# Scoring the third layer's sliding window in 64-row blocks, and unread matmuls in the last layer

## The chip, the cores and the metric

The kernel runs on one core of a Trainium2 chip. The metric is the device time of one launch in microseconds. A core has engines with queues of their own that run side by side: TensorE (PE) multiplies matrices and writes PSUM, ScalarE (ACT) evaluates the exponential here and reads PSUM, VectorE (DVE) does the elementwise work, GpSimd (POOL) and SyncE (SP) mostly issue transfers. An engine takes its instructions in program order; semaphores make one wait for another. [...]

## The reference

Four attention layers on one sequence of 2048 tokens of width 640, 32 heads of 20 elements. Layers 0 and 2 (the first and third) see a window of 256 keys, layers 1 and 3 (the second and last) see all keys:

```python
def attend(x, wqkv, wo, mask):            # mask is None in layers 1 and 3
    q, k, v = split_heads(x @ wqkv)       # 32 heads, Dh = 20
    s = einsum("bhqd,bhkd->bhqk", q, k) * Dh ** -0.5
    if mask is not None: s = where(mask, s, -1e9)
    return join_heads(softmax(s) @ v) @ wo
idx = arange(2048)
window = (idx[:, None] - idx[None, :] >= 0) & (idx[:, None] - idx[None, :] < 256)
x = x + attend(layernorm(x), A_wqkv, A_wo, window)    # layer 0
x = x + attend(layernorm(x), B_wqkv, B_wo, None)      # layer 1
x = x + attend(layernorm(x), A_wqkv, A_wo, window)    # layer 2
x = x + attend(layernorm(x), B_wqkv, B_wo, None)      # layer 3
```

## The kernel before

The queries are cut into four chunks `c` of 512, the heads into eight groups `g` of four. A `Unit(l, c, g)` is the attention of one layer, chunk and head group; the head `j` of a group lies on partitions 32j to 32j+19. A unit is a list of banks. A bank is one PSUM bank of scores, 128 keys by up to 512 queries of one head: keys are on the partitions, queries on the columns. `window_banks(c)` lists the banks of a windowed unit: three for each head, each filled by two score matmuls, of which one takes an early key block and the other a late one. For c > 0 all three are 512 columns wide (1536 columns a head); for c = 0 they have 512, 384 and 256 (1152).

Units of different layers follow each other in a fixed interleaved list. The eight units of layer 2 for a chunk stand, two at a time, between units of layer 1 of the next chunk; those of layer 2's last chunk stand between units of layer 3. The first part of layer 3, chunk 0, begins there; chunks 1 to 3 of layer 3 stand alone at the end, 24 units.

The main loop makes a "tile" of three banks (at times two or four) in each turn. For tile t it emits, in this order:

1. the score matmuls (line 1308) into one of two sets of PSUM banks, 0 to 2 for even tiles and 3 to 5 (with 6 for a tile of four banks) for odd ones;
2. the exponentials (line 1339), one ACTIVATE for each run of banks that begin at the same column, from PSUM to a bf16 tile `pt`;
3. other work by credit: `pump` advances generators for layer norm, projections (lines 364 and 465), output projection (line 552) and softmax normalisation, at a pace that `rate(t)` takes from due times counted in tiles; the pace is a number of TensorE microseconds a tile;
4. `keep_clock`: as long as the "heat" of the turn (matmuls of such other work) is under `state["least"]`, it emits an unread matmul, `unread` (line 634) into bank 6, or, when that bank is taken, "owes" one that goes ahead of the next tile's scores into its bank (line 1302). It multiplies the identity with a mask and nobody reads what it writes. `least` is 1.76 for a tile of three banks from layer 1 on, and zero from unit (3, 1, 0) on;
5. the products with the values (line 1373) for four banks of an earlier tile, accumulated in bank 7;
6. a step of the "side": some banks of layers 1 and 3 have their exponential evaluated by VectorE from polynomials (lines 910 to 941), at a pace of `SIDE_RATE` or 0.4 VectorE microseconds a tile;
7. the multiplication by 0/1 masks of the previous tile's windowed banks (line 1410, VectorE).

Tile t+1's scores go into the set that tile t-1's exponential has to release, while ACT works on tile t. `fill` in `t_tail` (line 1030) emits unread matmuls at the very end.

## Time and profile before

| what | value |
|---|---|
| time, median of 3 runs | 2285.77 us (2281.72 to 2287.35) |
| profiled span | 2282.3 us |
| ACT busy | 2169.6 us, 95% |
| PE busy | 1978.4 us, 87% |
| DVE busy | 1272.2 us, 56% |
| exponentials, line 1339 | 2096.5 us, 1638 recorded |
| unread matmuls, line 634 | 243.5 us, 708 recorded, none after 1653 us |
| window masks on DVE, line 1410 | 209.5 us, 403 recorded |

Busy time of an engine is the time in which at least one of its instructions was running; PE overlaps matmuls, so a busy PE isn't one at its peak. A few per cent of the matmuls can be missing from the records. PEclk is the share of TensorE's full clock that was granted.

### The profile page before, as it was taken

To read this page: it belongs to the slowest core of one execution; us is meant where nothing else is said; L and a number is where in the kernel's file an instruction comes from. 1 tells how busy PE (TensorE), PEld (TensorE's weight loads), DVE (VectorE), ACT (ScalarE), POOL (GpSimd) and SP (SyncE) were. 2 spreads that over 40 slices of the span, in tenths; PEclk is the share of its full clock that TensorE was granted. 3 is DMA by queue.
4 is the path that set the end of the run, shared out by engine and by line. 5 is a ranking of instruction groups with operands and counts; after the bars stand their busy time and mean duration, and the time that the engine had idled before them with its cause. 6 is when DMAs were issued, how large, how long until landed. Compare 5 with 4: busy or idle time off the path is not lost.

```text
span 2282.3 us, 40030 instructions
## 1 busy us (share of the span) xinstructions
PE 1978.4 (87%) x15586; PEld 704.1 (31%) x15746; DVE 1272.2 (56%) x2214; ACT 2169.6 (95%) x1741; POOL 271.0 (12%) x445
## 2 busy tenths in 40 slices
PE   8899999989898998888888998898878888888887
PEld 3343343333233333233332333232221122122222
DVE  6667675435454566455564643432555565666662
ACT  7789899999999999999899999999999999999997
POOL 4323223201100122001210022011000000000000
PEclk9899999999999999999999999999755565556556
DMA  6223223322210233002320043012111111111100
GB/s 193 78 69 101 81 83 90 97 75 56 70 33 14 61 96 93 15 27 64 101 71 14 16 116 95 28 44 74 54 47 30 30 42 30 30 39 41 35 17 15
DMA packets 88284, 135.16 MB, mean 59 GB/s; under 512 B 20766, under 2 KB 63486, under 8 KB 88094
## 3 DMA queue, kind: packets, MB, share of 16 engines
q1 hardware_dynamic: 68878, 79.43, 12.6%
q0 software_dynamic: 19216, 53.17, 7.8%
q8 instruction: 123, 2.02, 0.4%
q14 instruction: 67, 0.55, 0.1%
HBM read 99.52 MB, written 27.79 MB: 56 GB/s over the span
## 4 chain that ended last, share of the span: by engine, by line
ACT 45%; PE 30%; issue 16%; DVE 9%; DMA 0%; ACTq 0%; POOL 0%; SPq 0%; DVEq 0%; POOLq 0%
ACT pt L1339 44%; PE ps L1308 7%; PE ps L364 6%; PE ps L552 5%; PE ps L1373 4%; PE ps L465 3%; DVE pt L1410 2%; PE ps L634 1%; DVE st L314 1%; DVE on L1085 1%; ACT ka L1339 1%; PE ps L1081 1%; DVE x_sb L561 1%; PE ps L429 0%; DVE raw_o L910 0%
## 5 line engine op out<-in xcount | busy, mean ns | idle before, releaser
L1339 ACT ACTIVATE pt<-ps 128x1536 bf16<-128x1536 f32 (+2 forms) x1638 | 2096.5, 1478 | 74.2 <-PE ps L1308 64.9
L1308 PE MATMUL ps<-qt,kt 32*128 32x512 bf16 x4008 | 635.9, 451 | 176.7 <-ACT pt L1339 144.6
L1373 PE MATMUL ps<-pt,vt 128*21 128x512 bf16 x3852 | 462.5, 452 | 7.1 <-issue 4.5
L1308 PEld LDWEIGHTS <-kt 32*128 32x128 bf16 x4008 | 186.0, 93 | 594.1 <-issue 575.7
L1410 DVE TENSOR_TENSOR pt<-pt,masks 128x1024 bf16<-128x1024 bf16 (+6 forms) x403 | 209.5, 554 | 151.0 <-ACT pt L1339 150.5
L634 PE MATMUL ps<-masks,ident 128*128 128x512 bf16 x708 | 243.5, 387 | 27.7 <-DVE on L1085 7.1
L364 PE MATMUL ps<-xnT,wqk 128*128 128x512 bf16 x761 | 206.3, 382 | 19.2 <-DVE on L1085 3.9
L1373 PEld LDWEIGHTS <-vt 128*21 128x21 bf16 x3960 | 99.5, 90 | 337.4 <-issue 325.1
L314 DVE CAST st<-ps 128x512 bf16<-128x512 f32 x134 | 92.7, 692 | 183.8 <-PE ps L364 169.9
L552 PE MATMUL ps<-wop,on 128*128 128x320 bf16 x928 | 165.0, 317 | 8.3 <-DVE x_sb L561 5.2
L910 DVE TENSOR_SCALAR xnT<-ps 128x512 int32<-128x512 f32 x88 | 60.9, 692 | 185.8 <-PE ps L903 185.8
L1308 PE MATMUL ps<-qa,ka 32*128 32x384 bf16 (+2 forms) x1408 | 118.2, 278 | 27.7 <-ACT pt L1339 22.0
L1085 DVE TENSOR_TENSOR on<-on,ps 128x512 bf16<-128x512 bf16 x128 | 86.4, 685 | 65.8 <-PE ps L1081 64.7
L561 DVE TENSOR_TENSOR x_sb<-x_sb,ps 128x320 bf16<-128x320 bf16 x120 | 58.1, 484 | 115.1 <-PE ps L552 114.9
L857 DVE CAST on<-ps 128x512 bf16<-128x512 f32 x112 | 77.1, 688 | 75.1 <-PE ps L1373 48.3
L465 PE MATMUL ps<-wv,xnT 128*128 128x320 bf16 x640 | 110.6, 301 | 7.9 <-DVE on L1085 3.1
L552 PEld LDWEIGHTS <-on 128*128 128x128 bf16 x928 | 84.0, 101 | 77.0 <-issue 47.8
L364 PEld LDWEIGHTS <-wqk 128*128 128x128 bf16 x830 | 69.9, 97 | 111.3 <-issue 53.9
L634 PEld LDWEIGHTS <-ident 128*128 128x128 bf16 x798 | 59.7, 96 | 132.6 <-issue 131.2
L398 POOL TENSOR_SCALAR rstd<-mv 128x4 f32<-128x4 f32 x15 | 4.1, 277 | 776.6 <-DVE mv L385 755.9
L1373 PE MATMUL ps<-pt,va 128*21 128x384 bf16 (+2 forms) x1408 | 75.6, 282 | 3.9 <-DVE pt L1410 1.6
L1308 PEld LDWEIGHTS <-ka 32*128 32x128 bf16 x1408 | 43.0, 92 | 95.9 <-issue 85.9
(101 smaller groups left out, 1585.1 us busy)
## 6 DMA issues: line engine op xcount, KB each, us to landing
vt<-v_d SPq DMA_DIRECT2D x48, 336.0 KB
kt<-k_d SPq DMA_DIRECT2D x192, 80.0 KB
wqk<-in_B_wqkv_dram POOLq DMA_DIRECT2D x80, 160.0 KB, 3.5
wqk<-in_A_wqkv_dram POOLq DMA_DIRECT2D x70, 160.0 KB, 3.4
k_d<-st POOLq DMA_DIRECT2D x75, 128.0 KB, 2.1
q_d<-st POOLq DMA_DIRECT2D x75, 128.0 KB, 2.1
qt<-q_d SPq DMA_DIRECT2D x384, 20.0 KB
v_d<-vs POOLq DMA_DIRECT2D x16, 336.0 KB, 3.0
```

The source lines that it names most:

```text
L314: nc.vector.tensor_copy(out=out_, in_=in_)
L364: nc.tensor.matmul(pq, lhsT=wt[:, dc, :], rhs=xt[:, dc, :], start=(dc == 0), stop=(dc == KD - 1),)
L465: nc.tensor.matmul(pv, lhsT=xt[:, dc, i * P : (i + 1) * P], rhs=wv_sb[l % 2][:, dc, h * HD : (h + 1) * HD], start=(dc == 0), stop=(dc == K ...
L552: nc.tensor.matmul(yp, lhsT=on[:, g, qb * P : (qb + 1) * P], rhs=wop[:, g, i * HD : (i + 1) * HD], start=(g == a), stop=(g == b - 1),)
L561: nc.vector.tensor_tensor(out=xv, in0=had, in1=yp, op=ALU.add)
L634: nc.tensor.matmul(ps[:, b, :], lhsT=ident[:], rhs=masks[:, 0, :], start=True, stop=True)
L857: nc.vector.tensor_copy(out=oT, in_=op)
L1085: nc.vector.tensor_tensor(out=oT, in0=oT, in1=zb, op=ALU.mult)
L1308: nc.tensor.matmul(sp[:, i, col * P : (col + qn) * P], lhsT=u.k(kc, j), rhs=u.q(j, q0, qn), start=True, stop=True,)
L1339: nc.scalar.activation(out=pt[:, i:k, b0 * P :], in_=sp[:, i:k, b0 * P :], func=ACT.Exp, scale=SCALE,)
L1373: nc.tensor.matmul(op[32 * j : 32 * j + VW, q0 * P : (q0 + qn) * P], lhsT=u.v(kc, j), rhs=pg[:, i, col * P : (col + qn) * P], start=(first ...
L1410: nc.vector.tensor_tensor(out=pt_[:, i:k, cols], in0=pt_[:, i:k, cols], in1=mv_, op=ALU.mult)
```

## The change

Layer 2 alone gets a new list of banks, `windows(c)`. Keys are taken in blocks of 64 instead of 128: in a bank the lower 64 partitions hold one key block and the upper 64 the next one, each with the query columns that it needs, so less of the bank is outside the window. For c > 0 a head has two "fine" banks of 512 columns and one unmasked of 256 (1280 columns); for c = 0 two of 448 and one of 128 (1024). Each score matmul now has 64 key columns as weights and writes 64 partitions, and a lower and an upper one alternate. In a few columns the upper half belongs to other queries than the lower one; `mask` copies those columns, multiplied by a triangle, into a small tile `phi`, and they get value products of their own.

Layer 0 keeps the old banks (`wide_windows`). The heat that a tile must have follows its width in columns and not its number of banks, and no longer ends at the last layer, so unread matmuls go on to the end. They read the identity, repeated four times, instead of a mask. The side's pace goes from 0.85 to 1.05 and from 0.4 to 0.65 a tile. The core of the diff:

```diff
-SIDE_RATE = 0.85
+SIDE_RATE = 1.05
...
+    for n, ge, base in ((0, False, 0), (1, True, 0), (2, True, B), (3, False, -B)):
+        v = tri[:, n, :]
+        nc.gpsimd.affine_select(
...
-            ps[:, b, :], lhsT=ident[:], rhs=masks[:, 0, :], start=True, stop=True
+            ps[:, b, :].rearrange("p (a b) -> p a b", a=4), lhsT=ident[:], rhs=idents,
+            start=True, stop=True,
...
+    def windows(c):
+        found = []
+        for o in range(2):
+            k, q = 4 * c + o, 2 * o
+            low = [(k, q, 5, 1), (k + 2, q + 4, 2, 6)]
+            high = [(k, q + 1, 5, 2), (k + 2, q + 5, 1, 7)]
+            values = [
+                (k, q, 5, 1, False), (k + 2, q + 4, 2, 6, False), (k, q + 5, 1, 6, True),
+            ]
+            if c > 0:
+                low.append((k - 2, q, 1, 0))
+                high.insert(1, (k - 2, q, 2, 0))
+                values = [(k - 2, q, 1, 0, False), *values, (k - 2, q + 1, 1, 1, True)]
+            else:
+                high[0] = (k, q, 6, 1)
+            found.append(((0 if c > 0 else B, C), "fine", low, high, values))
+        pairs = [(4 * c + 2, 6, 2, 0)] + [(4 * c - 1, 0, 2, 2)] * (c > 0)
+        found.append(((0, 2 * B * len(pairs)), None, pairs, pairs, [(*p, False) for p in pairs]))
...
-                for n in range(2):
-                    for i, (u, j, m, b0, subs, first, last, end) in enumerate(cur):
-                        for kc, q0, qn, col in subs[n : n + 1]:
+                for n in range(0, max(len(x) for x in jobs), 2):
+                    for i, x in enumerate(jobs):
+                        for half, lhsT, rhs, col in (job for job in x[n : n + 2] if job):
+                            rows = slice(0, P) if half is None else slice(B * half, B * half + B)
                             nc.tensor.matmul(
-                                sp[:, i, col * P : (col + qn) * P],
-                                lhsT=u.k(kc, j), rhs=u.q(j, q0, qn), start=True, stop=True,
+                                sp[rows, i, col : col + rhs.shape[1]],
+                                lhsT=lhsT, rhs=rhs, start=True, stop=True,
...
-                state["least"] = warmth * n_b / 3 if state["unit"] < index[3, 1, 0, None] else 0.0
+                state["least"] = warmth * width / 3
...
+                if all(b[2] is not None and b[2] != "side" and b[2].masked in ("fine", None) for b in cur):
+                    r *= width / 2.5
...
-                side["credit"] = min(side["credit"] + (SIDE_RATE if side["late"] else 0.4), 1.2)
+                side["credit"] = min(side["credit"] + (SIDE_RATE if side["late"] else 0.65), 1.2)
```

In a tile that mixes banks of layer 2 with banks of layer 1 or 3, the latter are also scored in two halves of 64 keys.

More of the change, by code (lines that the diff above doesn't have):

```diff
@@ L28 @@
 HD = D // 2
+B = 64
 VW = DH + 1
@@ L72 @@
     ptp = pool("ptp", 6)
+    phip = pool("phip", 3)
     stp = pool("stp", 4)
@@ L95 @@
     spread4 = big.tile([64, 4, P], BF16, name="spread4", tag="spread4")
+    tri = big.tile([P, 4, B], BF16, name="tri", tag="tri")
     masks = big.tile([P, 3, C], BF16, name="masks", tag="masks")
@@ L155 @@
         )
+    nc.gpsimd.memset(tri[:], 1.0)
+    for n, ge, base in ((0, False, 0), (1, True, 0), (2, True, B), (3, False, -B)):
+        v = tri[:, n, :]
+        nc.gpsimd.affine_select(
+            out=v, in_=v, compare_op=ALU.is_ge if ge else ALU.is_gt, fill=0.0,
+            base=base, pattern=[[1 if ge else -1, B]], channel_multiplier=-1 if ge else 1,
+        )
+    idents = ident[:].unsqueeze(1).to_broadcast((P, 4, P))
     nc.vector.memset(ka_all[:, G:KA, :], 0.0)
@@ L674, in __init__ @@
             if self.windowed:
-                sets = [(m, b0, subs, j) for m, b0, subs in window_banks(c) for j in range(4)]
+                sets = [(w, w.cols, w.values, j) for w in (windows if l == 2 else wide_windows)(c) for j in range(4)]
             else:
@@ L681, in __init__ @@
                 sets = [
-                    (None, 0, [(kc, 0, 4, 0)], j) for kc in range(k0, k1) for j in range(4)
+                    (None, (0, C), [(kc, 0, C, 0, False)], j)
+                    for kc in range(k0, k1) for j in range(4)
                     if kc < NT - 1 or j not in self.aside
@@ L686, in __init__, with k, scores @@
             self.banks = [
-                (self, j, m, b0, subs, i < 4, i >= n - 4 + len(self.aside), i == n - 1)
-                for i, (m, b0, subs, j) in enumerate(sets)
-            ]
-        def k(self, kc, j):
+                (self, j, w, cols, subs, i < 4, i >= n - 4 + len(self.aside), i == n - 1)
+                for i, (w, cols, subs, j) in enumerate(sets)
+            ]
+        def k(self, kc, j, half=None):
+            o = kc * P
             if self.windowed:
-                t, o = ka[kc // 4, self.g], kc % 4
+                t, o = ka[kc // 4, self.g], o % C
             else:
-                t, o = kt[self.l, self.c, self.g], kc
-            return t[32 * j : 32 * j + 32, o * P : (o + 1) * P]
+                t = kt[self.l, self.c, self.g]
+            n = P
+            if half is not None:
+                o, n = o + half * B, B
+            return t[32 * j : 32 * j + 32, o : o + n]
         def q(self, j, q0, qn):
             t = qa[self.c, self.g] if self.windowed else qt[self.l, self.c, self.g]
-            return t[32 * j : 32 * j + 32, q0 * P : (q0 + qn) * P]
+            return t[32 * j : 32 * j + 32, q0 : q0 + qn]
+        def scores(self, j, w, subs):
+            if w is not None:
+                jobs = [
+                    (half, self.k(kc, j, half), self.q(j, q0, qn), col)
+                    for half, kc, q0, qn, col in w.scores
+                ]
+                if w.scores[0][0] is None:
+                    jobs = [x for job in jobs for x in (job, None)]
+                return jobs
+            return [
+                (half, self.k(kc, j, half), self.q(j, q0, qn), col)
+                for kc, q0, qn, col, _ in subs for half in range(2)
+            ]
         def v(self, kc, j):
@@ L706, in v, with __init__, wide_windows @@
             return vt[self.l, self.c, self.g][:, o : o + VW]
-    def window_banks(c):
+    class Window:
+        def __init__(self, cols, masked, scores, values):
+            self.cols, self.masked, self.scores, self.values = cols, masked, scores, values
+    def wide_windows(c):
+        k = 4 * c - 2
         if c > 0:
-            k = 4 * c - 2
-            return [
+            sets = [
                 (0, 0, [(k, 0, 1, 0), (k + 3, 1, 3, 1)]),
@@ L716, in window_banks @@
             ]
-        return [
-            (2, 0, [(0, 0, 3, 0), (3, 3, 1, 3)]),
-            (0, 1, [(1, 1, 3, 1)]),
-            (1, 2, [(2, 2, 2, 2)]),
+        else:
+            sets = [
+                (2, 0, [(0, 0, 3, 0), (3, 3, 1, 3)]),
+                (0, 1, [(1, 1, 3, 1)]),
+                (1, 2, [(2, 2, 2, 2)]),
+            ]
+        return [
+            Window(
+                (P * b0, C), m,
+                [(None, kc, P * q0, P * qn, P * col) for kc, q0, qn, col in subs],
+                [(kc, P * q0, P * qn, P * col, False) for kc, q0, qn, col in subs],
+            )
+            for m, b0, subs in sets
+        ]
+    def windows(c):
[6 more added lines that the diff above has]
+                (k, q, 5, 1, False), (k + 2, q + 4, 2, 6, False), (k, q + 5, 1, 6, True),
+            ]
+            if c > 0:
+                low.append((k - 2, q, 1, 0))
+                high.insert(1, (k - 2, q, 2, 0))
+                values = [(k - 2, q, 1, 0, False), *values, (k - 2, q + 1, 1, 1, True)]
+            else:
+                high[0] = (k, q, 6, 1)
+            found.append(((0 if c > 0 else B, C), "fine", low, high, values))
+        pairs = [(4 * c + 2, 6, 2, 0)] + [(4 * c - 1, 0, 2, 2)] * (c > 0)
+        found.append(((0, 2 * B * len(pairs)), None, pairs, pairs, [(*p, False) for p in pairs]))
+        return [
+            Window(
+                cols, masked,
+                [
+                    (half, kc, B * q0, B * qn, B * col)
+                    for both in zip(low, high) for half, (kc, q0, qn, col) in enumerate(both)
+                ],
+                [(kc, B * q0, B * qn, B * col, hi) for kc, q0, qn, col, hi in values],
+            )
+            for cols, masked, low, high, values in found
         ]
@@ L904, in t_side @@
                             ps[:, 6, :], lhsT=u.k(NT - 1, u.aside[2 * pair + i]),
-                            rhs=u.q(u.aside[2 * pair + i], 0, 4), start=True, stop=True,
+                            rhs=u.q(u.aside[2 * pair + i], 0, C), start=True, stop=True,
                         )
@@ L1030, in fill @@
                 nc.tensor.matmul(
-                    ps[:, 0, :], lhsT=ident[:], rhs=masks[:, 0, :], start=True, stop=True
+                    ps[:, 0, :], lhsT=ident[:], rhs=idents, start=True, stop=True
                 )
@@ L1219 @@
             if u.aside and len(at) < 2 and banks[n + 1][0] is u and len(tiles) >= 3 * len(at) + (at or [0])[0]:
-                extra = [(u, u.aside[len(at)], "side", 0, [(NT - 1, 0, 4, 0)], False, False, False)]
+                extra = [
+                    (u, u.aside[len(at)], "side", None, [(NT - 1, 0, C, 0, False)], False, False, False)
+                ]
                 at.append(len(tiles))
@@ L1258, in rate, with mask @@
             return min(1.1 * r, 1.0 if u.l == 0 else 0.9)
+        def mask(pt, hi, i, k, first):
+            v = pt[:, i:k, :]
+            n = k - i
+            (ps_, pn), (ss, _), _ = v.ap
+            if "t" not in hi:
+                hi["t"] = phip.tile([P, 3, 2, B], BF16, name="phi", tag="phi")
+            w = v.rearrange("p n (b e) -> p n b e", e=B)
+            nc.vector.tensor_tensor(
+                out=hi["t"][:, i:k, int(first) :, :], in0=w[:, :, 6 if first else 1 : 7 : 5, :],
+                in1=tri[:, 3:4, :].unsqueeze(1).to_broadcast((P, n, 2 - first, B)), op=ALU.mult,
+            )
+            if first:
+                for a, b in ((1, 3), (5, 8)):
+                    x = v[:, :, a * B : b * B]
+                    m = tri[:, 3 - (b - a) : 3, :].rearrange("p b e -> p (b e)")
+                    nc.vector.tensor_tensor(
+                        out=x, in0=x, in1=m.unsqueeze(1).to_broadcast((P, n, (b - a) * B)),
+                        op=ALU.mult,
+                    )
+                return
+            x = bass.AP(v.tensor, v.offset, [(ps_, pn), (ss, n), (5 * B, 2), (1, 3 * B)])
+            m = tri[:, 0:3, :].rearrange("p b e -> p (b e)")
+            nc.vector.tensor_tensor(
+                out=x, in0=x,
+                in1=m.unsqueeze(1).unsqueeze(1).to_broadcast((P, n, 2, 3 * B)), op=ALU.mult,
+            )
         last_tick[0] = len(tiles)
@@ L1302 @@
                     nc.tensor.matmul(
-                        sp[:, 0, :], lhsT=ident[:], rhs=masks[:, 0, :], start=True, stop=True
-                    )
-                for n in range(2):
-                    for i, (u, j, m, b0, subs, first, last, end) in enumerate(cur):
-                        for kc, q0, qn, col in subs[n : n + 1]:
+                        sp[:, 0, :].rearrange("p (a b) -> p a b", a=4), lhsT=ident[:],
+                        rhs=idents, start=True, stop=True,
+                    )
+                if any(b[2] is not None and b[2] != "side" for b in cur):
+                    jobs = [b[0].scores(b[1], None if b[2] == "side" else b[2], b[4]) for b in cur]
+                else:
+                    jobs = [
+                        [(None, b[0].k(b[4][0][0], b[1]), b[0].q(b[1], 0, C), 0)] for b in cur
+                    ]
+                for n in range(0, max(len(x) for x in jobs), 2):
+                    for i, x in enumerate(jobs):
+                        for half, lhsT, rhs, col in (job for job in x[n : n + 2] if job):
+                            rows = slice(0, P) if half is None else slice(B * half, B * half + B)
                             nc.tensor.matmul(
-                                sp[:, i, col * P : (col + qn) * P],
-                                lhsT=u.k(kc, j), rhs=u.q(j, q0, qn), start=True, stop=True,
+                                sp[rows, i, col : col + rhs.shape[1]],
+                                lhsT=lhsT, rhs=rhs, start=True, stop=True,
                             )
@@ L1334 @@
                 while i < n_b:
-                    b0 = cur[i][3]
+                    a, e = cur[i][3]
                     k = i
-                    while k < n_b and cur[k][3] == b0:
+                    while k < n_b and cur[k][3] == (a, e):
                         k += 1
                     nc.scalar.activation(
-                        out=pt[:, i:k, b0 * P :], in_=sp[:, i:k, b0 * P :],
-                        func=ACT.Exp, scale=SCALE,
+                        out=pt[:, i:k, a:e], in_=sp[:, i:k, a:e], func=ACT.Exp, scale=SCALE,
                     )
                     i = k
+                hi = {}
                 for i, b in enumerate(cur):
-                    pts.append((t, pt, i, b))
+                    pts.append((t, pt, i, b, hi))
+                width = sum(b[3][1] - b[3][0] for b in cur) / C
                 warmth = 1.76 if state["unit"] >= woven else 1.0
-                state["least"] = warmth * n_b / 3 if state["unit"] < index[3, 1, 0, None] else 0.0
+                state["least"] = warmth * width / 3
                 state["floor"] = 0.9 if state["unit"] >= index[1, 1, 0, None] else 0.0
@@ L1369 @@
                     require(("v", u.l, u.c, 1))
-                for m, (kc, q0, qn, col) in enumerate(subs):
-                    for _, pg, i, b in group:
+                for m, (kc, q0, qn, col, high) in enumerate(subs):
+                    for _, pg, i, b, ph in group:
                         j = b[1]
+                        src = ph["t"][:, i, col // (5 * B), :] if high else pg[:, i, col : col + qn]
                         nc.tensor.matmul(
-                            op[32 * j : 32 * j + VW, q0 * P : (q0 + qn) * P],
-                            lhsT=u.v(kc, j), rhs=pg[:, i, col * P : (col + qn) * P],
+                            op[32 * j : 32 * j + VW, q0 : q0 + qn],
+                            lhsT=u.v(kc, j), rhs=src,
                             start=(first and m == 0), stop=(last and m == len(subs) - 1),
@@ L1393 @@
             if n_b:
-                side["credit"] = min(side["credit"] + (SIDE_RATE if side["late"] else 0.4), 1.2)
+                side["credit"] = min(side["credit"] + (SIDE_RATE if side["late"] else 0.65), 1.2)
                 side_step(False)
             if t > 0 and masked is not None:
-                cur_, pt_ = masked
+                cur_, pt_, hi_ = masked
+                kinds = [
+                    (b[2].masked, b[3]) if b[2] is not None and b[2].masked is not None else None
+                    for b in cur_
+                ]
                 i = 0
                 while i < len(cur_):
-                    m, b0 = cur_[i][2:4]
                     k = i
-                    while k < len(cur_) and cur_[k][2] == m:
+                    while k < len(cur_) and kinds[k] == kinds[i]:
                         k += 1
-                    if m is not None:
-                        cols = slice(max(b0, m == 1) * P, 3 * P if m == 1 else C)
-                        mv_ = masks[:, m, cols].unsqueeze(1).to_broadcast(
-                            (P, k - i, cols.stop - cols.start)
-                        )
-                        nc.vector.tensor_tensor(
-                            out=pt_[:, i:k, cols], in0=pt_[:, i:k, cols], in1=mv_, op=ALU.mult
-                        )
+                    if kinds[i] is not None:
+                        m, (a, e) = kinds[i]
+                        if m == "fine":
+                            mask(pt_, hi_, i, k, a > 0)
+                        else:
+                            if m == 1:
+                                a, e = max(a, P), 3 * P
+                            v = pt_[:, i:k, a:e]
+                            mv = masks[:, m, a:e].unsqueeze(1).to_broadcast((P, k - i, e - a))
+                            nc.vector.tensor_tensor(out=v, in0=v, in1=mv, op=ALU.mult)
                     i = k
-            masked = (cur, pt) if n_b else None
+            masked = (cur, pt, hi) if n_b else None
         mfree.update((b, (0, 0)) for b in range(1, 6))
```

## The prediction

> **What bounds the kernel now.** First the page's busy times and its strip of 40 slices (57 us each).

> ```profile
> PE 1978.4 (87%) x15586; PEld 704.1 (31%) x15746; DVE 1272.2 (56%) x2214; ACT 2169.6 (95%) x1741; POOL 271.0 (12%) x445
> ...
> ACT  7789899999999999999899999999999999999997
> ...
> PEclk9899999999999999999999999999755565556556
> ```

> ACT is full from about 456 us to the end, save the last slice; only the first 400 us, where layer 0 is projected, show digits of 7 and 8. PEclk falls from full to about half at slice 29 (1653 us), where layer 3's chunks 1 to 3 begin and the unread matmuls stop; ACT stays at 9 there.

> Second, the waits. For the whole run, then for 855 to 985 us (a stretch with eight units of layer 2), then for 1600 to 2268 us (the last layer alone):

> ```profile
> ACT pt L1339 <- PE ps L1308: 64.9, 131, 2.6
> ```
> ```profile
> ACT pt L1339 <- PE ps L1308: 0.3, 2, 0.2
> ```
> ```profile
> ACT pt L1339 <- PE ps L1308: 10.4, 15, 1.6
> ```

> ACT waits for scores 64.9 us in all, but 0.3 us in 130 us where layer 2 runs, and 10.4 us in the 668 us of the last layer. The same view gives 0.9, 0.4 and 0.2 us for the other three stretches with layer 2 (585 to 640, 1133 to 1262, 1393 to 1484 us). So the time of layer 2 is ACT's work, and the last layer has about 10 us to win, plus its end.

> Third, ACT's timeline in the last layer, for a price:

> ```profile
> 1894.65 23.10 ACT L1339 ACTIVATE pt<-ps 128x1536 bf16<-128x1536 f32 x17
> 1917.32 2.20 ACT L1339 ACTIVATE ka<-ps 128x2048 bf16<-128x2048 f32 x1
> 1919.09 12.52 ACT L1339 ACTIVATE pt<-ps 128x1536 bf16<-128x1536 f32 x9
> 1931.17 2.21 ACT L1339 ACTIVATE ka<-ps 128x2048 bf16<-128x2048 f32 x1
> ```

> Start to start, 17 tiles of 1536 columns take 22.67 us and nine take 12.08: 34.75 / 26 = 1.337 us each. A tile of 2048 takes 1919.09 - 1917.32 = 1.77. The difference, 0.43 us for 512 columns, is 0.84 ns a column; what is left of 1.337 is about 0.05 us for the instruction. The page's mean of 1478 ns is of no use here: recorded exponentials overlap.

> Fourth, PE's timeline at full clock, in a pure stretch of layer 1 and in one of layer 2:

> ```profile
> 692.90 0.39 PE L1308 MATMUL ps<-qt,kt 32*128 32x512 bf16 x3 [0.41 <-ACT pt L1339]
> 693.22 0.60 PE L634 MATMUL ps<-masks,ident 128*128 128x512 bf16 x2
> 693.76 0.40 PE L1373 MATMUL ps<-pt,vt 128*21 128x512 bf16 x4
> ```
> ```profile
> 861.23 0.40 PE L1308 MATMUL ps<-qa,ka 32*128 32x384 bf16 x6 [0.85 <-ACT pt L1339]
> 862.52 0.40 PE L1373 MATMUL ps<-pt,va 128*21 128x128 bf16 x8
> ```

> Three scores of 512 columns side by side take 0.39 us, and so do six of 128 and 384; four or eight value products take 0.40. A second unread matmul adds 0.60 - 0.39 = 0.21 us: that is 512 columns of stream. PE still idles 0.41 us before the first group and 0.85 us before the layer 2 group, waiting for ACT to release the bank.

> [...] The trace shows rows alone (three scores) and columns alone (four value products), never both at once, as the new scores need. [...]

> **The change, part by part.**

> *Exponentials of layer 2.* A head loses 1536 - 1280 = 256 columns in chunks 1 to 3 and 1152 - 1024 = 128 in chunk 0: 32 x (3 x 256 + 128) = 28,672 columns, at 0.833 ns 23.9 us. Tiles that mix widths need more instructions: the two programs hold 1665 and 1699 exponentials, 34 x 0.05 = 1.7 us[...]. Net 22 us, on the engine that sets the pace in all four stretches: on the path.

> *Scores of layer 2.* A fine bank has six matmuls for two: 320, 128 and 64 columns for the lower half and the same for the upper. If the halves run side by side, a tile streams 512 columns as before. If not, 1024: +0.21 us. Weights: 18 loads of 64 columns a tile for six of 128 that were hidden within 0.39 us; by columns 1152 to 768, up to 0.39 x 1.5 = 0.58 us, so +0.19. [...] I take +0.2, which the idle 0.41 to 0.85 us before the scores holds. Behind a late score on PE stand the tile's projections and value products, and ACT waits for the score itself. What doesn't hide is the tile of three 256-column banks: ACT needs only 768 x 0.833 + 50 = 0.69 us for it, and PE must bring the next tile's scores, 0.4 to 0.6 us from the release. I put 0.1 to 0.2 us on each of 32 units: +4 us; both ends, 0 and +24 (rival one).

> *Value products.* Twelve a head for six, 1536 columns as before; four heads run side by side and weights are 21 columns. Eight took 0.40 us, twenty in five steps should take 0.5 to 0.6; in the same idle time. No cost.

> *Masks.* By forms, DVE took 953 ns for 1536 elements and 419 for 512: 0.52 ns an element and 0.15. A unit of chunks 1 to 3 had 3.6 us (2 x 0.953, 4 x 0.419). Now two tiles with 0.35 for `phi` and 0.75, and one with 0.28 and 0.55: 3.0 us. Nothing on the path; DVE is at 56%.

> *Unread matmuls.* The program goes from 868 of them in lines 634 and 1302 to 1579: 711 more at 0.21 us, nearly all in the last layer, about 1.5 a tile; 445 of the additional ones stand ahead of scores. At the half clock of before the scores took 0.61 us and ACT was still 159.9 us busy of 160; now two unread ones and the scores need 0.43 + 0.39 = 0.82 us after the release, of a tile's 1.34. I expect full clock and no new wait inside units. What it wins are the waits at chunk ends, where output projections ran at half clock: half of 10.4, -5 us, and at the end, after the last exponential (2267 us), the products, normalisation and projection that run in about 3 us of PE time at half clock: -1.5 us.

> *The rest.* The other operand of unread matmuls has the same 512 columns: nothing. The side's faster pace moves DVE work within a unit and adds none; DVE has the room: nothing. Five GpSimd instructions for `tri` ahead of the first statistics: about 1 us on an engine that had 0.5 us idle there: +0.5. `width` gives layer 0's chunk 0 fewer unread matmuls: nothing.

> Sum: -22 + 4 - 5 - 1.5 + 0.5 = -24; 2285.8 - 24 = 2262 us.

> **The rivals.** *One: PE becomes the bound in layer 2.* Some 96 tiles hold fine banks; if [...]a projection or unread matmul takes part of the idle time, 0.25 us a tile is left over: +24, 2262 - 4 + 24 = 2282 us. [...] Against: 0.41 to 0.85 us idle. *Two, slower than before: the unread matmuls cost the last layer.* Some 480 tiles; if each loses 0.08 us because PE reaches the scores late, +38, and the gain at chunk ends is gone: 2262 + 6.5 + 38 = 2306 if none of it hides, 2297 with a quarter hidden. For it: 445 of them precede scores. Against: the 0.82 us of 1.34, and between 1140 and 1596 us the same load runs with ACT full. *Three: more is won.* No stall in layer 2 and all of the last layer's 10.4 us: -22 - 10.4 - 2 = 2251 us.

> **How the numbers follow.** Forecast 0.68, rival one 0.14, two 0.10, three 0.08. 0.3% is 6.9 us, so faster is under 2278.9: forecast, three and a third of one, 0.81. Within: the rest of one and a little of two, 0.11. Slower: 0.08. The range goes from 2249, most of rival three, to 2281, most of rival one.

> **What would show it.** Right: exponentials that add up to 28,672 columns less and some 20 us less ACT busy time before 1500 us; waits of ACT for scores that stay under some 2 us in each stretch of layer 2; PEclk near full to the end; waits of about 5 us in the last layer, with exponentials still 1.34 us apart. Wrong: score groups of fine tiles well over 0.6 us with ACT waiting behind them (rival one); idle ACT time inside the last layer's units, next to unread matmuls ahead of scores (rival two).

## The result, and the profile after

The changed kernel takes 2311.92 us, the median of 4 runs (2311.08 to 2321.03); the kernel before takes 2286.56 us. The ratio is 1.0121, with a 95% interval of 1.0089 to 1.0153: slower by about 25 us, where 24 us less was forecast. The profiled executions have spans of 2319.3 us (after) and 2282.3 us (before): 37 us apart, because the profiled execution of the kernel after is the longest of its four.

The page of the kernel after, busy times and two rows of its strip (40 slices of 58 us):

```profile
PE 2055.4 (89%) x18259; PEld 762.9 (33%) x18339; DVE 1261.0 (54%) x2274; ACT 2158.8 (93%) x1775; POOL 274.0 (12%) x450
...
ACT  7789898899989999999899999999999999999998
...
PEclk9899998899979999999998999999999999999999
```

PEclk is now full in the last layer, as forecast (1.00 in the slices of 57 us from 1596 us on, 0.97 in three of them). But, counted from 0, it has digits of 7 and 8 at slices 6, 7, 11 and 21, where before showed 9, and ACT shows 8 at 6, 7 and 11, where before it had 9, 8 and 9. The sums say the same over the stretch from 130 to 1600 us (columns: stretch, its length, busy time of PE, PEld, DVE, ACT and POOL with instruction counts, PEclk, DMA share, GB/s), and over the 57 us from 627 us. Before, then after:

```profile
130.00:1600.00 1470.00, 1309.10 (x11137) 505.10 (x11281) 787.89 (x1479) 1419.28 (x1132) 227.65 (x352) 1.00 0.24 66
627.00:684.00 57.00, 51.28 (x426) 17.75 (x433) 32.70 (x62) 56.33 (x55) 0.00 (x0) 1.00 0.11 33
```
```profile
130.00:1600.00 1470.00, 1330.18 (x12764) 521.55 (x12831) 766.79 (x1514) 1363.70 (x1133) 226.66 (x348) 0.96 0.23 64
627.00:684.00 57.00, 51.84 (x434) 16.83 (x423) 27.64 (x56) 48.69 (x41) 0.00 (x0) 0.81 0.10 28
```

A mean clock of 0.96, made of stretches at full and at half clock, is 0.04 x 2 x 1470 = 118 us at half clock; the clock's records give 116.1 us, in 13 stretches of 3.4 to 23.9 us. Before had none between 130 and 1600 us. In the 57 us around one such stretch ACT works 48.69 us of 57, before 56.33. (The kernel after is then some 25 us behind, so the two aren't at the same work.)

ACT's waits for scores (total, times, longest). Of the kernel after, from 0 to 460, 460 to 1640 and 1640 to 2320 us:

```profile
ACT pt L1454 <- PE ps L1423: 46.4, 69, 3.3
```
```profile
ACT pt L1454 <- PE ps L1423: 62.1, 115, 2.4
```
```profile
ACT pt L1454 <- PE ps L1423: 5.7, 12, 1.3
```

Of before, from 0 to 420, 420 to 1640 and 1640 to 2283 us:

```profile
ACT pt L1339 <- PE ps L1308: 25.9, 40, 2.6
```
```profile
ACT pt L1339 <- PE ps L1308: 29.7, 77, 1.2
```
```profile
ACT pt L1339 <- PE ps L1308: 9.2, 14, 1.6
```

So the work on ACT did go (the two programs' exponentials differ by exactly the forecast 28,672 columns), and after 1640 us, where the last layer runs, there was a gain; but before that ACT waits about 53 us more for TensorE. ACT's busy time falls by 10.8 us only, 2158.8 for 2169.6: an exponential of 1536 columns after a wait counts 1.45 us and one in a row 1.33, and there are 64 more waits in the whole run (195 for 131), which makes some 8 us less of a fall.

Milestones, before and after: layer 0's last scores start at 382.6 and 395.5 us, the first scores of layer 2 come at 589.9 and 614.3 us, its last ones at 1479.5 and 1521.6; from there to the last chunk's first output transfer 797.3 and 792.2 us pass. 24 us are lost before layer 2 starts, another 18 across it.

How one such fall of the clock looks, on PE's timeline of the kernel after (start, length, what, and in brackets the idle time before it and what ended it):

```profile
659.21 0.39 PE L645 MATMUL ps<-ident 128*128 128x512 bf16 x1
659.53 0.24 PE L1492 MATMUL ps<-pt,va 128*21 128x128 bf16 x4
659.79 0.26 PE L1423 MATMUL ps<-qa,ka 32*64 32x128 bf16 x6
...
661.85 0.53 PE L645 MATMUL ps<-ident 128*128 128x512 bf16 x1 [0.71 <-DVE rT L1141]
662.31 0.56 PE L1492 MATMUL ps<-pt,va 128*21 128x320 bf16 x8
...
662.85 0.61 PE L1423 MATMUL ps<-qt,kt 32*128 32x512 bf16 x3
```

and on ACT's:

```profile
657.27 4.83 ACT L1454 ACTIVATE pt<-ps 128x1344 bf16<-128x1344 f32 x6 [0.16 <-PE ps L1423]
663.57 1.45 ACT L1454 ACTIVATE pt<-ps 128x1536 bf16<-128x1536 f32 x1 [1.46 <-PE ps L1423]
666.29 1.45 ACT L1454 ACTIVATE pt<-ps 128x1536 bf16<-128x1536 f32 x1 [1.27 <-PE ps L1423]
```

The narrow banks are done quickly, 0.24 and 0.26 us for their matmuls above; then PE, in program order, waits 0.71 us in one unread matmul for a bank that VectorE still reads. At that point the same instructions begin to take 0.53 to 0.61 us instead of 0.39: the clock has halved, for 23.9 us, and in that time ACT waits 0.2 to 1.5 us ahead of most of its tiles.

### The profile page after: what moved, and what is told of

The parts are those of the page before. It is cut to its first block, busy times and chain, and to the rows that moved or that the text cites. A ratio compares the mean times of both kernels' runs of the same rounds, so it can differ in the third digit from the quotient of the medians.

```text
span 2319.3 us, 45507 instructions
## 1 busy us (share of the span) xinstructions
PE 2055.4 (89%) x18259; PEld 762.9 (33%) x18339; DVE 1261.0 (54%) x2274; ACT 2158.8 (93%) x1775; POOL 274.0 (12%) x450
## 4 chain that ended last, share of the span: by engine, by line
ACT 35%; PE 35%; DVE 14%; issue 14%; POOL 1%; DMA 1%; SPq 0%; ACTq 0%; DVEq 0%; POOLq 0%
ACT pt L1454 33%; PE ps L1423 9%; PE ps L375 6%; PE ps L1492 6%; PE ps L645 4%; PE ps L563 4%; PE ps L476 3%; DVE on L1162 2%; ACT ka L1454 1%; DVE st L325 1%; PE ps L1409 1%; DVE xnT L1010 1%; DVE xnT L1006 1%; DVE xnT L1002 1%; PE ps L1158 1%
## 5 line engine op out<-in xcount | busy, mean ns | idle before, releaser
L1454 ACT ACTIVATE pt<-ps 128x1536 bf16<-128x1536 f32 (+3 forms) x1669 | 2077.5, 1391 | 123.6 <-PE ps L1423 114.0
L1423 PE MATMUL ps<-qt,kt 32*128 32x512 bf16 (+1 forms) x4066 | 558.6, 392 | 59.5 <-ACT pt L1454 48.1
L645 PE MATMUL ps<-ident 128*128 128x512 bf16 x1064 | 376.1, 401 | 43.0 <-DVE on L1162 12.7
L1492 PE MATMUL ps<-pt,vt 128*21 128x512 bf16 x3840 | 399.5, 393 | 2.9 <-issue 1.5
L1423 PEld LDWEIGHTS <-kt 32*128 32x128 bf16 (+1 forms) x4066 | 161.7, 91 | 443.7 <-issue 421.1
L1409 PE MATMUL ps<-ident 128*128 128x512 bf16 x515 | 169.6, 387 | 70.9 <-ACT pt L1454 50.8
L563 PE MATMUL ps<-wop,on 128*128 128x320 bf16 x928 | 158.6, 305 | 10.0 <-DVE x_sb L572 6.2
L1423 PE MATMUL ps<-qa,ka 32*64 32x128 bf16 (+5 forms) x2560 | 122.2, 252 | 21.5 <-ACT pt L1454 18.5
L645 PEld LDWEIGHTS <-ident 128*128 128x128 bf16 x1064 | 81.5, 97 | 179.5 <-issue 172.0
L1536 DVE TENSOR_TENSOR pt<-pt,masks 128x1024 bf16<-128x1024 bf16 (+7 forms) x211 | 105.7, 534 | 14.6 <-ACT pt L1454 14.5
L1347 DVE TENSOR_TENSOR phi<-pt,tri 128x384 bf16<-128x384 bf16 (+4 forms) x112 | 32.0, 286 | 145.0 <-ACT pt L1454 138.1
```

The source lines that it names most:

```text
L563: nc.tensor.matmul(yp, lhsT=on[:, g, qb * P : (qb + 1) * P], rhs=wop[:, g, i * HD : (i + 1) * HD], start=(g == a), stop=(g == b - 1),)
L645: nc.tensor.matmul(ps[:, b, :].rearrange("p (a b) -> p a b", a=4), lhsT=ident[:], rhs=idents, start=True, stop=True,)
L1409: nc.tensor.matmul(sp[:, 0, :].rearrange("p (a b) -> p a b", a=4), lhsT=ident[:], rhs=idents, start=True, stop=True,)
L1423: nc.tensor.matmul(sp[rows, i, col : col + rhs.shape[1]], lhsT=lhsT, rhs=rhs, start=True, stop=True,)
L1454: nc.scalar.activation(out=pt[:, i:k, a:e], in_=sp[:, i:k, a:e], func=ACT.Exp, scale=SCALE,)
L1492: nc.tensor.matmul(op[32 * j : 32 * j + VW, q0 : q0 + qn], lhsT=u.v(kc, j), rhs=src, start=(first and m == 0), stop=(last and m == len(sub ...
```

## The experiments

**The operand of the unread matmuls.** First theory: an identity has few nonzero elements, and the clock depends on them. `e1_mask_operand` is the kernel after with the old operand at all three places; `e2_ident_in_before` and `e3_repeat_mask_in_before` put the repeated identity, and a mask repeated in the same pattern, into the kernel before, at two of the three places. One of the places:

```diff
-            ps[:, b, :].rearrange("p (a b) -> p a b", a=4), lhsT=ident[:], rhs=idents,
+            ps[:, b, :], lhsT=ident[:], rhs=masks[:, 0, :], start=True, stop=True
```

> The changed kernel, its unread matmuls reading the mask again instead of the identity; nothing else differs. Theory A ([...]the clock drops between 200 and 1540 us are its doing): PEclk 1.00 from 171 us to the end, about 2262 us as forecast. Theory B (the narrow matmuls of the 64-row blocks let the clock drop, whatever the unread ones read): clock drops stay, about 2310 us.

> The kernel before, its unread matmuls reading the identity four times as in the change; nothing else differs. Theory A: half-clock stretches appear between 171 and 1600 us, 20 to 50 us more, 2305 to 2335 us. Theory B: 2286 us, clock as before.

> The kernel before, its unread matmuls reading the first 128 columns of the mask (about half ones) four times, with the same repeated access pattern as the identity in the change. Theory A in its form 'what the data are': as before, 2286 us, no half clock between 171 and 1600 us. If it is the repeated pattern that matters: as e2, 2305 to 2335 us. Theory B: 2286 us.

Measured: 2318.63 us, ratio 1.0154 (1.0126 to 1.0182); 0.9999 (0.9988 to 1.001); 0.9998 (0.9989 to 1.0007). Neither the data nor the pattern shows a cost. The theory falls. The traces of e2 and e3 each have 10.2 us at half clock between 130 and 1600 us, in three stretches, where the one of before has none; the time is the same. Falls of that size come and go.

**Unread matmuls in the last layer, alone**, in the kernel before:

```diff
-                state["least"] = warmth * n_b / 3 if state["unit"] < index[3, 1, 0, None] else 0.0
+                state["least"] = warmth * n_b / 3
```

> The kernel before with unread matmuls (reading the mask) to the end of the last layer; nothing else differs. The forecast's terms for the last layer: 5 us of waits and 1.5 us at the end less, about 2279 us, PEclk near 1.00 after 1653 us. Rival two (late scores): ACT idle inside the units of the last layer, 2290 us or more.

Measured: 2276.27 us, 0.9958 (0.9943 to 0.9973). That is 9 us less. This part of the change is a gain, and the loss lies in the others.

**Three parts undone.** `e5_layer0_unsplit` scores layer 1's banks that share a tile with layer 0's in one matmul again. (In the program the halves were to be for layer 2's tiles, but 19 of layer 0's groups take them as well.) `e6_layer0_unsplit_heat_by_banks` is e5 with the heat by number of banks. `e7_old_side_pace` is the kernel after with the old pace of the side, and `e8_three_undone` is all three.

```diff
-                if any(b[2] is not None and b[2] != "side" for b in cur):
+                if any(b[2] is not None and b[2] != "side" and b[2].scores[0][0] is not None for b in cur):
...
-                state["least"] = warmth * width / 3
+                state["least"] = warmth * n_b / 3
...
-SIDE_RATE = 1.05
+SIDE_RATE = 0.85
...
-                side["credit"] = min(side["credit"] + (SIDE_RATE if side["late"] else 0.65), 1.2)
+                side["credit"] = min(side["credit"] + (SIDE_RATE if side["late"] else 0.4), 1.2)
```

> The changed kernel, but a bank of layer 1 that shares a tile with the wide banks of layer 0 is scored in one matmul again; tiles with the fine banks of layer 2 keep the halves. Theory S (the halves put a second array shape into tiles of layer 0, their streams no longer overlap, about 0.3 us of PE each in a stage that PE bounds, and the clock drops there follow): layer 0 ends at about 383 us instead of 395, 12 to 20 us less in all, 2292 to 2300 us. If the halves are harmless: 2312 us.

> As e5, and the heat that a tile must have follows its number of banks again, so narrow tiles of layer 2 get more unread matmuls. Theory H (after the fine units the clock drops because the heat by width keeps too few unread matmuls there): no half clock after the fine units, 15 to 25 us less than e5. If the drops come from the fine matmuls themselves whatever the heat: as e5.

> The changed kernel with the side's paces of before (0.85 and 0.4). If the faster pace keeps VectorE from releasing bank 6 in time: 5 to 15 us less than 2312. If it only moves work: 2312 us.

> The changed kernel with all three of these: layer 0 unsplit, heat by banks, old side paces. What stays is layer 2's windows in 64-row blocks and the unread matmuls of the last layer. If theories S and H name the cause: about 2262 us as forecast, clock full from 130 us on. If the fine matmuls themselves cost the time: 2285 us or more.

| kernel | us | range | ratio to before (95%) |
|---|---|---|---|
| e5 | 2315.25 | 2308.19 to 2321.43 | 1.013 (1.0101 to 1.0158) |
| e6 | 2293.7 | 2291.25 to 2297.44 | 1.0038 (1.0023 to 1.0053) |
| e7 | 2289.33 | 2279.6 to 2316.75, 20 runs | 1.0029 (1.0009 to 1.0049) |
| e8 | 2283.86 | 2271.07 to 2291.83, 20 runs | 0.9992 (0.9983 to 1.0002) |

The halves in layer 0 don't show in the time, although the last scores of e5's layer 0 start at 384.6 us and not 395.5: e5 is 4 us behind the kernel before at the first scores of layer 2, and 26 us behind at its last. The heat by width costs about 21 us (e5 to e6), the side's pace about 23 (after to e7). The parts don't add: the pace is worth 23 us undone first, but 10 us after the heat (e6 to e8). ACT's waits for scores fall in step, after, e5, e6, e8: 114.0, then

```profile
ACT pt L1459 <- PE ps L1428: 110.2, 195, 2.6
```
```profile
ACT pt L1459 <- PE ps L1428: 91.9, 170, 3.1
```
```profile
ACT pt L1459 <- PE ps L1428: 80.8, 153, 3.1
```

and so does the half clock between 130 and 1600 us: 116.1, 112.6, 37.5, 34.1 us. e7 shows the tie without any edit: over its executions, the longest left out, the mean clock ran from 0.986 (2279.6 us) to 0.968 (2313.07 us), and a straight line through these 19 has 18.5 us for each 0.01 (correlation -0.99). 0.01 of the mean clock over 2290 us is 46 us at half clock, so each such microsecond goes with 0.40 us of time. The kernel after has a median clock of 0.974 against e7's 0.981, which is 13 us on that line; it is 22.6 us slower. So some 10 us of the side's pace in the kernel after don't go with the clock. A correlation alone doesn't say whether the stall or the clock comes first.

**The side's pace, alone.** `e9_side_pace_in_before` puts both new rates into the kernel before; `e13_side_early_065` and `e14_side_late_105` one each.

```diff
-SIDE_RATE = 0.85
+SIDE_RATE = 1.05
...
-                side["credit"] = min(side["credit"] + (SIDE_RATE if side["late"] else 0.4), 1.2)
+                side["credit"] = min(side["credit"] + (SIDE_RATE if side["late"] else 0.65), 1.2)
```

> The kernel before with the side's faster paces (1.05 and 0.65), nothing else. If the pace itself costs (e7 gained 23 us by undoing it in the changed kernel): 2290 to 2305 us. If it costs only where the clock is near its edge, as in the changed kernel: 2286 us within 4.

> The kernel before with the side's early pace at 0.65 (0.85 in the last layer stays). If the early rate carries e9's 21 us (VectorE's polynomial steps come closer together, PE waits for bank 6 and the clock drops between 480 and 1640 us): 2298 to 2305 us. If it is the late rate: 2286 us.

> The kernel before with the side's late pace at 1.05 (0.4 stays). By the waits of ACT in the last layer, which are 3 to 5 us longer with the faster pace in e9 and in the changed kernel: 2289 to 2292 us. If the late rate carries e9's cost: 2300 us or more.

Measured: 2306.94 us, 1.0084 (1.0064 to 1.0104); 2297.21 us, 1.0063 (1.004 to 1.0086); 2290.95 us, 1.002 (1.0011 to 1.0029). Of 21 us for both, about 12 come from the rate before the last layer and 5 from the other. Two of PE's waits from 450 to 1640 us, in e9 and then in before:

```profile
PE ps L634 <- DVE on L1085: 7.2, 19, 1.0
PE ps L634 <- DVE vs L314: 5.5, 4, 2.4
```
```profile
PE ps L634 <- DVE on L1085: 4.2, 14, 0.8
PE ps L634 <- DVE vs L314: 0.4, 1, 0.4
```

With more polynomial work at once on VectorE, projections lie in PSUM longer (our reading of these waits), and the unread matmul that wants their bank waits, up to 2.4 us, with all of PE's queue behind it. The matmul that is there to keep the clock up is then what stops PE. One of these waits, in e9:

```profile
817.61 0.59 PE L634 MATMUL ps<-masks,ident 128*128 128x512 bf16 x1 [2.12 <-DVE vs L314]
```

At 817.3 us, within this pause, the clock falls. Here the stall comes first. Before has no pause of PE as long as 1 us between 260 and 1600 us. e9 has 41.0 us at half clock between 130 and 1600 us, before 0. One of its falls, at 465.8 us, comes before the side has begun, with the instructions of before: not every fall is the pace's doing.

**The blocks, with most of the rest as before.** `e11_layer2_windows_alone` is e8 with the unread matmuls ending at the last layer again; `e10_more_heat_in_layer2` is e8 with more of them in layer 2's tiles; `e12_no_pump_in_narrow_tiles` is e8 with little projection work in narrow tiles. One more part of the change stays in all of these: in tiles with banks of layer 2 alone the pace of other work is multiplied by the width over 2.5 banks, which is 1.2 for three full ones. No run undoes it alone.

```diff
-                state["least"] = warmth * n_b / 3
+                state["least"] = warmth * n_b / 3 if state["unit"] < index[3, 1, 0, None] else 0.0
...
-                state["least"] = warmth * n_b / 3
+                state["least"] = warmth * n_b / 3 * (1.35 if any(b[0].l == 2 for b in cur) else 1.0)
...
-                    r *= width / 2.5
+                    r *= width / 2.5 if width > 2.9 else 0.25
```

> e8 without the unread matmuls of the last layer: the kernel before with the 64-row blocks in layer 2 and nothing else of weight. By e8 (2284) and e4 (9 us less by the last layer's unread matmuls): 2293 us, so the blocks alone cost 7 us where the forecast has them win 18. If the two don't add: 2286 us or less.

> e8 with 1.35 times the heat in every tile that holds a bank of layer 2, so more unread matmuls there. If what e8 still loses against the forecast (2284 against 2262 us) is mainly half clock after the fine units: no half clock between 130 and 1600 us, 2268 to 2276 us. If it is mainly ACT waiting at full clock after the narrow tiles: 2282 us or more, since unread matmuls only add to PE's queue.

> e8 with the pace of other work cut to a quarter in tiles of layer 2 narrower than three full banks (and left at width / 2.5 in full ones). If ACT's waits after the narrow tiles (about 0.5 us a unit, 15 us in all, at full clock) come from projections queued on PE ahead of the next scores: these waits fall by half or more, 2272 to 2278 us. If they come from the many small score and value matmuls themselves: 2284 us, as e8.

Measured: e11 2289.84 us, 1.002 (1.0008 to 1.0032); e10 2289.46 us, 1.0011 (0.9994 to 1.0028); e12 2275.07 us (2274.91 to 2281.35), 0.9958 (0.9944 to 0.9973). The blocks alone cost 4 us instead of bringing 18. More unread matmuls don't cure it. Two things eat the gain. The first is the clock again: e8's two falls between 130 and 1600 us, at 716.4 and 917.8 us, come with two of its longest waits of unread matmuls for the instruction that is L1085 in before, where no such wait is over 0.8 us:

```profile
714.24 0.38 PE L645 MATMUL ps<-ident 128*128 128x512 bf16 x1 [1.52 <-DVE on L1162]
```
```profile
918.72 0.59 PE L645 MATMUL ps<-ident 128*128 128x512 bf16 x1 [1.65 <-DVE on L1162]
```

No run takes out these waits alone. The second thing shows on PE's timeline of e8, at full clock:

```profile
870.07 0.39 PE L375 MATMUL ps<-xnT,wqk 128*128 128x512 bf16 x1
871.06 0.42 PE L1428 MATMUL ps<-qa,ka 32*64 32x128 bf16 x16 [0.59 <-ACT pt L1459]
871.63 0.81 PE L375 MATMUL ps<-xnT,wqk 128*128 128x512 bf16 x3 [0.16 <-issue]
872.38 0.40 PE L1497 MATMUL ps<-pt,va 128*21 128x64 bf16 x12
872.60 0.23 PE L1497 MATMUL ps<-phi,va 128*21 128x64 bf16 x8
872.76 0.42 PE L1428 MATMUL ps<-qa,ka 32*64 32x320 bf16 x18
```

Between the start of one score group and the next lie 1.70 us. The scores themselves are quick, 0.42 us for 16 or 18 matmuls; three projections and 20 value products fill the rest. ACT spends 0.71 us on the narrow tile before (768 columns) and is done with the 1280 columns of the first group at 872.90; then it waits 0.43 us for the scores that PE started at 872.76. With turn lengths of before (1.33 us of ACT a tile) that queue had its time; now ACT's turns are shorter and PE's are not. A burst is a pair of layer 2's units, from its first scores to 4 us after its last. In the bursts ACT loses, at full clock, 5.7 us before, 20.7 in e8 and 20.5 in e11 (start to start, less the 50 ns and 0.833 ns a column that exponentials back to back take in these traces).

For e11 the two give an estimate: -22 us of columns and instructions, +15 us in the bursts, and +12 us for 30.7 us at half clock between 130 and 1600 us at the 0.40 above, together +5 for a measured +4.

e12 was to prove the second cause by thinning the queue: its time is less than e8's (the intervals don't touch, though all four executions lie in e8's range), but its burst losses are 21.3 us. Its median clock is 0.987 for e8's 0.983, which is 7 of the 9 us on e7's line. That projections are what holds the scores up is thus not shown.

**Chunk 0 in the old banks.** `e15_chunk0_in_wide_banks` is e12 with the blocks for c > 0 alone; `e16_chunk0_wide_mixed_slow` is e15 with the reduced pace in mixed tiles too.

```diff
-                sets = [(w, w.cols, w.values, j) for w in (windows if l == 2 else wide_windows)(c) for j in range(4)]
+                sets = [(w, w.cols, w.values, j) for w in (windows if l == 2 and c > 0 else wide_windows)(c) for j in range(4)]
...
-                if all(b[2] is not None and b[2] != "side" and b[2].masked in ("fine", None) for b in cur):
+                if any(b[0].l == 2 and b[0].c > 0 for b in cur):
```

> e12 with layer 2's chunk 0 in the old banks, chunks 1 to 3 in 64-row blocks. ACT gets 8 x 0.36 = 2.9 us more work. In e12's trace the four stretches of chunk 0 lose 8.3 us to waits at full clock, 1.4 in the kernel before. If these waits are the blocks' own: 3 to 6 us less than e12, about 2270 us. If not: 2278 us.

> e15, and the quarter pace also holds for narrow tiles in which a bank of layer 2 stands with banks of layer 1 or 3. In e12's trace the longest waits of ACT follow just these mixed tiles (0.4 to 1.3 us after the 1024-column exponential). If projections queued there are the cause: 2 to 5 us less than e15. If not: as e15.

Measured: 2275.08 us (2268.64 to 2281.67), 0.9952 (0.9938 to 0.9966); 2274.84 us, 0.9954 (0.9939 to 0.9969). The pace in mixed tiles changes nothing. Between 130 and 1600 us e15 has 6.8 us at half clock left. e15, e16, e12 and e4 all take about 2275 us, 9 to 11 us less than the kernel before, and can't be told apart: with the blocks in chunks 1 to 3 or without them the time is the same, and what they all have is the last layer's unread matmuls.

## Why the prediction was wrong, step by step

- *"So the time of layer 2 is ACT's work."* True of before, where the waits were near nothing. (Chunk 0's stretch goes on to 709 us and not 640; the rest of it has no such wait either.) It gave no measure of how far PE was from being the limit once ACT's turns got shorter. 28,672 columns went as forecast, and 0.833 ns a column is what exponentials back to back took in both traces (1536 columns in 1.330 us, 1024 in 0.904); the 22 us for them did not come through.
- *"The side's faster pace moves DVE work within a unit and adds none; DVE has the room: nothing."* This step failed most plainly: +21 us alone (e9). DVE at 56% had room on average, but PE's queue stands behind single copies out of PSUM on DVE, and these came later: unread matmuls waited up to 2.4 us for one that had cost 0.4 us.
- *"`width` gives layer 0's chunk 0 fewer unread matmuls: nothing."* It takes them from every narrow tile of layer 2 too, and costs about 21 us in the changed kernel (e5 to e6). With it undone the half clock between 130 and 1600 us went from 112.6 to 37.5 us. The working saw PEclk at 1.00 throughout (in every slice of 57 us from 171 to 1596 us) and took that as a given; these matmuls helped to hold it.
- *Stalls of the narrow tile, "+4 us; both ends, 0 and +24".* At full clock the bursts' loss grew from 5.7 to 15.6 us in the kernel after and to 20.7 in e8, +10 to +15 us; at half clock another 7.9 us are lost in after's bursts.
- *Rival one* ended at PE as the bound of layer 2, which it became after narrow tiles, but by another mechanism. Its 0.25 us a tile was the author's estimate. The weight loads, +0.2 us a tile in the working, don't show: 18 fine matmuls, each with its load, take 0.42 us in e8, three of 512 took 0.39 in before.
- *Unread matmuls, "-5 us" and "-1.5 us".* Right in kind: -9 us alone (e4), waits in after's last layer 5.7 us for the forecast 5. Rival two, that these would cost the last layer, is refuted.
- *Operand, masks, value products: nothing.* The operand is measured (e1 to e3), and nothing in after's waits points to masks. The value products weren't measured alone; they are part of the queue in a narrow turn.
- *"Waits of ACT for scores that stay under some 2 us in each stretch of layer 2"* was the test that fell first: the same view of the kernel after has 9.9, 4.8, 6.1 and 1.0 us. "PEclk near full to the end" fell in the middle of the run and held in the last layer, and ACT's busy time fell by 10.8 us where "some 20 us less" was named.

The singles, -9 (last layer), +21 (side), +4 (blocks) and +21 (heat by width), don't sum to +25. They seem to draw on one margin, and how much of a fall is chance (some 33 us of spread in e7) can't be shared out among them. Open also is what exactly delays the narrow tiles' scores, and how much of the loss would go with the waits of the unread matmuls for their bank.

## What to carry to other kernels

When the bounding engine's work gets shorter, ask whether the other engines' work in the same turn shrinks with it; compare both for the narrowest turn, and not the averages. A clock of 1.00 in the profile is no margin (before had it from 171 to 1596 us, and with the side's new pace alone it had 41.0 us at half clock): before removing or postponing matmuls, look for the longest pauses of PE, and treat one behind a late copy out of PSUM as a possible loss of the clock, also where the waiting matmul is one that should keep the clock up (in e9 the clock fell within such a pause, of 2.12 us). And undo an edit's parts one by one: here the smallest, unread matmuls in the last layer, held all of the gain that could be measured.

## What the runs showed of the hardware

```profile
228.96 0.59 PE L634 MATMUL ps<-masks,ident 128*128 128x512 bf16 x2 [2.05 <-DVE on L1085]
```
```profile
225.72 0.59 PE L634 MATMUL ps<-masks,ident 128*128 128x512 bf16 x2 [2.05 <-DVE on L1085]
...
227.94 1.03 PE L634 MATMUL ps<-masks,ident 128*128 128x512 bf16 x2
```

- That gives no threshold: in the kernel after, with the halves in layer 0, the clock fell with 1.05 and 1.01 us of this pause in two steps. The share of a step in which columns streamed (at 512 in 0.21 us, what one more unread matmul of 512 adds in before, 0.60 for 0.39) doesn't give one either: from 20 us on it was 0.15 to 0.53 ahead of falls in the kernel after, but steps from 0.38 up kept the full clock; the clock came back after shares of 0.66 to 0.92 at half clock, and stayed half after some of up to 0.91.
- Scores of 32 rows by 64 columns ran side by side: 18 of them, 3072 columns in all, in 0.42 us (e8); one after another at 0.21 us for 512 they would take 1.26 us, an estimate. Mixed in a tile with scores over all 128 columns, they didn't run beside those: in layer 0 of the kernel after, a group that began with the halves had its first wide one 0.33 us later and was done after 0.72 us at the earliest, where in before both kinds started within 0.01 us and such a group took 0.39.
- Exponentials of a PSUM source, back to back, took 0.833 ns a column and 50 ns at the least, for widths from 256 to 1536: 0.263, 0.903 and 1.330 us for 256, 1024 and 1536 columns in before, start to start.
